# Softmax sums by one reduction on VectorE, copies of the transposed weights on ScalarE

## The chip, the core and the metric

The kernel runs on one core of one Trainium2 chip. The metric is the time of one execution on the device, in microseconds; the median of several executions is compared. The engines named below are TensorE (PE in profile rows, and PEld for its loads of stationary operands), VectorE (DVE), ScalarE (ACT), GpSimd (POOL) and SyncE (SP), which issues most transfers.

## The reference

A block-sparse attention feeds two feed-forward blocks. Batch 4, 8 heads, 576 positions, head width 64, all in float32; cut to what matters:

```python
scores = scale * np.matmul(q, k.transpose(0, 1, 3, 2))
mask_local = (rel >= 0) & (rel < stride)                       # stride = 32, heads 0 to 3
mask_strided = (rel >= 0) & (pos[None, :] % stride == pos[:, None] % stride)   # heads 4 to 7
scores = np.where(masks[None, :, :, :], scores, -1000000000.0)
scores = scores - np.max(scores, axis=-1, keepdims=True)
attn = np.exp(scores)
attn = attn / (np.sum(attn, axis=-1, keepdims=True) + 1e-09)
x = np.matmul(attn, v)                     # then heads side by side: 2304 x 512
h = x @ moe_w_in                           # 512 -> 2048
x = (h * np.tanh(softplus(h))) @ moe_w_out
g, val = x @ moe2_w_gate, x @ moe2_w_val   # 512 -> 1536
out = (g * sigmoid(g) * val) @ moe2_w_out
```

## The kernel before

The attention runs in 24 steps, six per batch: three local steps of 6 tiles of scores 128 x 96, and three strided ones, two of 8 tiles 128 x 64 and one of 6. (A tile holds two blocks of 64 queries, one above the other.) In the first three batches the local steps come first, in the last one the strided ones. Most steps have two halves, written s.0 and s.1.

The order of the work in the attention stage is written out by hand as a list of words, `ORDER`, which one loop turns into instructions. Every engine executes its own instructions in the order of that list. The words of a step s are: `Qs` scores on TensorE, into two PSUM banks ("sc", two buffers, so the scores of step s+1 wait for the maxima of step s); `Ms.h` mask and row maximum on VectorE, one instruction and one reading of its accumulator per tile; `Es.h` exponentials on ScalarE, one per tile, each with its row sum in an accumulator (`accum_out`), whose reading is an instruction of its own; `As` the addition of 1e-9 to the sums on GpSimd; `Rs` the reciprocal on VectorE; `Ns.h` the normalization on GpSimd; `Ts.h` the transposes on TensorE into PSUM; `Cs.h` or `Ds.h` the copy of the transposed weights to SBUF, on VectorE or ScalarE; `Ps` weights times values on TensorE, into the one bank "tp" and, in strided steps, one of "xp"; `Hs` and `Os` the split of the result into a high part (ScalarE) and the rest (VectorE).

Between them stand the words of the first feed-forward block, which starts while the attention still runs: `g` (input matmuls, line 160), `p` (output matmuls), `a`, `b`, `m`, `gh`, `gl`, `y` (what lies between and behind them), `w`, `wh`, `wl`, `wg` (the conversion of weights, four steps each, mostly on VectorE), and `s` (a few matmuls on zeros). `L` and `V` are loads of queries and keys, and of values. Behind the list, from about 118 us, the rest of the two feed-forward blocks follows, three matmuls per product of high and low parts.

Of the kernel before, what the change touches and what calls it, by code (L numbers as in the profile page):

```python
# [62 lines left out]
ORDER = """  # L63
L0
Q0 M0.0 M0.1 E0.0 s4 L1 E0.1
Q1 L2 M1.0 M1.1 A0 E1.0 R0 N0.0 s4
Q2 N0.1 T0.0 M2.1 E1.1 T0.1 A1 M2.0 L3 C0.0 R1
Q3 N1.0 C0.1 E2.1 M3.0 E2.0 N1.1 M3.1 P0 A2 w E3.1 V0 H0 R2 L4 T1.0 T1.1 w s2 C1.0 w D1.1 E3.0 O0 s3 N2.0 N2.1
Q4 w w P1 A3 R3 V1 M4.0 T2.1 wh M4.1 H1 T2.0 N3.0 O1 L5 D2.1
Q5 E4.0 s4 C2.0 P2 N3.1 T3.1 C3.1 w wg E4.1 T3.0 H2 M5.0 w g0.0.0 M5.1 L6  # L70
Q6 A4 R4 w D3.0 N4.0 E5.0 O2 V2 E5.1 w N4.1 M6.1 P3 L7 wh w A5 R5 T4.0 T4.1 M6.0 H3 E6.1 E6.0 g0.0.1 N5.1 C4.0 g0.1.0
Q7 w N5.0 wg O3 D4.1 g0.1.1 T5.0 A6 M7.0 g0.2.0 V3 D5.0 T5.1 w w R6 wh P4 H4 g0.2.1 w D5.1 N6.0 wg M7.1 O4 V4 L8
Q8 E7.0 P5 T6.0 g0.1.2 M8.0 g0.0.2 H5 M8.1 E7.1 O5 N6.1 w E8.0 A7 R7 T6.1 E8.1 C6.1 L9 C6.0 g0.0.3 w b0.0
Q9 P6 N7.1 M9.0 H6 A8 N7.0 wh R8 T7.1 N8.0 V5 M9.1 E9.0 E9.1 L10 g0.1.3 g0.3.0 V6 T7.0 O6
Q10 C7.1 w C7.0 M10.0 M10.1 E10.1 T8.0 E10.0 w C8.0 N8.1 wg L11 w A9 g0.3.1 T8.1 R9
Q11 P7 L12 g0.2.2 H7 N9.0 N9.1 g0.2.3 C8.1 T9.1 M11.0 A10 M11.1 a0.2 R10 b0.1 E11.0 E11.1 V7 C9.1 O7 N10.0 N10.1 A11
T10.1 g0.3.2 T9.0
Q12 M12.1 C10.1 P8 w H8 O8 T10.0 w D9.0 wh L13 g0.3.3 E12.1 g1.0.0 R11 P9 M12.0
Q13 H9 C10.0 N11.0 N11.1 w wg M13.0 M13.1 b0.3 T11.1 D11.1 O9 g1.2.0 g1.0.1 V8 E12.0 g1.2.1 E13.0 A12 w T11.0 L14 V9
P10  # L80
Q14 w R12 L15 M14.0 C11.0 N12.1 H10 E13.1 O10 w N12.0 g1.1.0 g1.1.1 M14.1 E14.0 g1.1.2 P11 T12.0 H11 w E14.1 O11 C12.0
A14 m0.0 V10 wh g1.0.2 w A13 gh0.0 R13 R14 g1.2.2 g1.0.3 g1.1.3 a1.0 N13.0 T12.1 g1.2.3 a1.1 N13.1 g1.3.0 g1.3.1 m0.1
m0.3 w V11 N14.1
Q15 C12.1 gh0.1 wl m0.2 P12 L16 m1.0 H12 gl0.0 w a1.2 T13.0 T13.1 m1.1 D13.0 g1.3.2 gh0.3 p0.2.0 g1.3.3 gl0.1 w gh1.1
M15.0 p0.0.0 p0.0.1 m1.2 C13.1 wh a1.3 M15.1 gh0.2 N14.0 w p0.1.0 wl
Q16 M16.1 T14.1 T14.0 L17 M16.0 m1.3 p0.2.1 w p0.1.1 E15.1 E15.0 wh V12 O12
Q17 gl0.2 A15 E16.0 P13 gl0.3 L18 E16.1 R15 wl C14.0 V13 M17.1 C14.1 p0.0.2 N15.1 H13 M17.0 N15.0 A16 T15.1 p0.1.2
E17.0 O13 p0.2.2 R16 p0.0.3 p0.1.3 p0.2.3 T15.0
Q18 y0.0 y0.2 N16.0 N16.1 M18.1 P14 E17.1 H14 T16.0 A17 R17 C15.0 L19 p0.3.0 E18.1 y0.1 O14 V14 g2.0.0 D15.1 M18.0
p0.3.1 T16.1 C16.0 E18.0 N17.0 P15 N17.1  # L90
Q19 H15 w T17.1 p0.3.2 L20 g2.2.0 M19.1 D17.1 V15 p0.3.3 A18 R18 O15 E19.1 M19.0 gh1.0 T17.0 C16.1 g2.0.1
Q20 C17.0 N18.1 P16 N18.0 L21 y0.3 V16 M20.0 E19.0 T18.1 T18.0 w H16 gh1.3 M20.1 A19 g2.1.0 g2.1.1 D18.1 R19 O16
Q21 N19.0 N19.1 P17 D18.0 T19.0 g2.2.1 w E20.0 H17 g2.0.2 M21.1 T19.1 E20.1 A20 gl1.1 gh1.2 M21.0 g2.2.2 O17 tbl
g2.1.2 R20 gl1.0 g2.0.3 L22
Q22 C19.0 b2.0 P18 N20.0 E21.1 N20.1 H18 T20.1 gl1.2 g2.3.0 w D20.1 E21.0 g2.2.3 V17 A21 g2.1.3 g2.3.1 L23 b2.2 O18
D19.1 M22.1 R21 b2.1 T20.0 g2.3.2 p1.0.0 P19 C20.0 M22.0
Q23 w E22.1 V18 E22.0 N21.0 A22 H19 N21.1 gl1.3 T21.0 M23.1 O19 V19 p1.0.1 E23.1 C21.0 M23.0 g2.3.3 b2.3 p1.1.0 w
E23.0 wh w P20 T21.1 A23 H20 C21.1 p1.0.2 p1.0.3 p1.3.0 m2.3 O20 R22 p1.1.1 p1.1.2 P21 N22.0 T22.0 w wl m2.2 H21 O21
y1.0 R23 p1.3.1 N22.1 gh2.2 N23.1 V20 D22.0 p1.3.2 N23.0 T22.1 D22.1 p1.2.0 gl2.2 p1.2.1 m2.1 P22 T23.0 m2.0 H22
O22 p1.1.3 gh2.0 T23.1 y1.1 gl2.0 wh D23.1 gh2.1 p1.2.2 V21 p1.3.3 p1.2.3 gl2.1 D23.0 P23 V22 H23 O23 gh2.3 wg y1.3  # L100
gl2.3 V23 y1.2
# [1823 lines left out]
```

## Time and profile before

| what | value |
|---|---|
| median of 3 executions | 850.07 us (849.73 to 850.78) |
| the profiled execution | 850.62 us |
| its span, first to last instruction | 848.8 us |
| outside the span | 1.82 us |
| TensorE busy (ends of matmuls modelled) | 840.2 us, 99% |
| VectorE busy | 688.8 us, 81% |
| ScalarE busy | 478.5 us, 56% |
| GpSimd busy | 218.6 us, 26% |

The span is what the rows of the profile cover; what lies around it belongs to the time but to no row. Shares are averages over stages of quite different kinds: the attention stage is the first 118 us of 849.

### The profile page before, as it was taken

How to read it: one execution, taken by the hardware profiler on the slowest of the kernel's cores; microseconds unless marked ns; L12 is line 12 of the kernel's file. 1: busy time of each engine (PE TensorE's matmuls, PEld its weight loads, DVE VectorE, ACT ScalarE, POOL GpSimd, SP SyncE). 2: the span in 40 equal slices, each digit the busy share in tenths (PEclk: the TensorE clock that was granted, in tenths of full speed). 3: DMA queues.
4: the chain of work that ended last, by engine and by line, in shares of the span. 5: the costliest groups of instructions: out<-in, count | busy, mean ns of one | idle time of the engine just before them, and what ended most of it. 6: DMA issues, size and time to landing. Idle time of an engine off the chain costs nothing.

```text
span 848.8 us, 14459 instructions
## 1 busy us (share of the span) xinstructions
PE 840.2 (99%) x5177; PEld 699.7 (82%) x5177; DVE 688.8 (81%) x1442; ACT 478.5 (56%) x1128; POOL 218.6 (26%) x229
## 2 busy tenths in 40 slices
PE   8999999999999999999999999999999999999998
PEld 5778778888888888888888888888888878888886
DVE  6999879687677737687588999999999788677977
ACT  7999965575647547572736535353444534545353
POOL 5552221002000010101222121220205634334253
PEclk9999999999999999999999999999999999999999
DMA  9875353625957494873266655665575777669722
GB/s 283 264 228 167 105 185 158 247 85 115 306 137 218 105 274 138 186 287 144 89 258 223 225 192 198 217 211 206 192 265 181 234 239 222 231 189 249 199 75 100
DMA packets 50184, 166.08 MB, mean 196 GB/s; under 512 B 5440, under 2 KB 9408, under 8 KB 47808
## 3 DMA queue, kind: packets, MB, share of 16 engines
q1 hardware_dynamic: 42480, 133.48, 46.0%
q0 software_dynamic: 6480, 24.12, 12.4%
q10 hardware_dynamic: 1152, 7.55, 2.4%
q8 instruction: 41, 0.67, 0.3%
q14 instruction: 31, 0.25, 0.1%
HBM read 108.51 MB, written 56.62 MB: 195 GB/s over the span
## 4 chain that ended last, share of the span: by engine, by line
PE 92%; DVE 4%; DMA 2%; issue 1%; ACT 1%; POOL 0%; SPq 0%; DVEq 0%; ACTq 0%
PE y L160 23%; PE h L160 8%; PE o L160 8%; PE cX L160 8%; PE cXg L160 7%; PE cXv L160 7%; PE c L160 4%; PE cZ L160 4%; PE cZg L160 4%; PE cZv L160 4%; PE oX L160 3%; PE cY L160 2%; DMA qk<-in_qk_dram 2%; PE xp L599 2%; PE tp L562 2%; PE cYg L160 2%
## 5 line engine op out<-in xcount | busy, mean ns | idle before, releaser
L160 PE MATMUL y<-g,w 128*128 128x512 f32 (+1 forms) x960 | 202.3, 369 | 0.0
L160 PEld LDWEIGHTS y<-g,w 128*128 128x128 f32 x960 | 166.7, 189 | 29.7
L155 POOL TENSOR_TENSOR fs<-k,fs 128x512 fp32r<-128x512 f32 x24 | 37.5, 1569 | 139.9 <-ACT fs L150 127.8
L1143 POOL DMA_DIRECT2D yd<-yv x20 | 16.0, 802 | 187.3 <-ACT yv L1137 187.3
L160 PE MATMUL h<-xh,w 128*128 128x512 f32 (+1 forms) x208 | 61.5, 360 | 0.0
L516 ACT ACTIVATE pt<-pt,sm 128x64 f32<-128x64 f32 (+1 forms) x160 | 55.9, 361 | 3.7 <-DVE sm L502 3.7
L160 PE MATMUL o<-fs,wr 128*128 128x512 f32 x240 | 56.2, 390 | 0.0
L160 PE MATMUL cXg<-T,wr 128*128 128x512 f32 x216 | 54.8, 389 | 0.0
L160 PE MATMUL cXv<-T,wr 128*128 128x512 f32 x216 | 54.8, 389 | 0.0
L160 PEld LDWEIGHTS o<-fs,wr 128*128 128x128 f32 x240 | 44.7, 188 | 9.1
L160 PEld LDWEIGHTS cXv<-T,wr 128*128 128x128 f32 x216 | 40.6, 188 | 8.4
L160 PEld LDWEIGHTS cXg<-T,wr 128*128 128x128 f32 x216 | 40.5, 188 | 8.4
L1581 ACT COPY k<-cXg 128x512 f32<-128x512 f32 x18 | 10.6, 587 | 59.5 <-PE cXg L160 59.3
L160 PEld LDWEIGHTS h<-xh,w 128*128 128x128 f32 x208 | 37.0, 189 | 6.2 <-issue 1.2
L1137 ACT COPY yv<-y 128x512 f32<-128x512 f32 x40 | 23.2, 589 | 28.6 <-PE y L160 26.2
L545 POOL TENSOR_TENSOR pt<-pt,sm 128x192 f32<-128x192 f32 (+2 forms) x48 | 34.1, 730 | 18.1 <-DVE sm L538 13.1
L160 PE MATMUL h<-xl,w 128*128 128x512 f32 (+1 forms) x104 | 36.4, 350 | 0.0
L160 PE MATMUL c<-yh,wr 128*128 128x256 f32 x192 | 35.5, 283 | 0.0
L1590 ACT ACTIVATE k<-k 128x512 f32<-128x512 f32 x27 | 17.1, 633 | 31.1 <-DVE k L1586 31.1
L160 PE MATMUL cX<-xT,w 128*128 128x512 f32 x144 | 34.6, 389 | 0.0
L155 POOL TENSOR_TENSOR fs<-t,fs 128x512 fp32r<-128x512 f32 x20 | 28.5, 1431 | 22.6 <-ACT fs L150 13.6
L155 POOL TENSOR_TENSOR fs<-s,fs 128x512 fp32r<-128x512 f32 x18 | 26.4, 1468 | 27.8 <-ACT fs L150 27.8
(243 smaller groups left out, 2150.6 us busy)
## 6 DMA issues: line engine op xcount, KB each, us to landing
raw<-in_w_dram SPq DMA_DIRECT2D x44, 512.0 KB, 4.7
rawl<-in_w_dram SPq DMA_DIRECT2D x24, 512.0 KB, 4.3
yd<-yv POOLq DMA_DIRECT2D x20, 512.0 KB, 5.9
wr<-wd_p SPq DMA_DIRECT2D x18, 512.0 KB, 4.6
wr<-wd_g_S SPq DMA_DIRECT2D x16, 512.0 KB, 3.4
wr<-wd_v_S SPq DMA_DIRECT2D x14, 512.0 KB, 4.8
wr<-wd_g_W SPq DMA_DIRECT2D x10, 512.0 KB, 6.3
wd_v_W<-wr SPq DMA_DIRECT2D x10, 512.0 KB, 5.4
```

Of the source, the lines that this page charges most:

```text
L155: eng.tensor_tensor(out=lo, in0=src, in1=hi.bitcast(F32), op=ALU.subtract)
L160: nc.tensor.matmul(o, lhsT=lhs, rhs=rhs, start=first and i == 0, stop=last and i == 2, skip_group_check=more)
L516: nc.scalar.activation(out=pt[:, x], in_=pt[:, x], func=AF.Exp, scale=-1.0, bias=sm[:, 0, x:x + 1], accum_out=sm[:, 1, x:x + 1],)
L545: nc.gpsimd.tensor_tensor(out=a, in0=a, in1=sm[:, 1, x].unsqueeze(2).to_broadcast(a.shape), op=ALU.mult)
L562: nc.tensor.transpose(tp[:, 128 * x:128 * x + 128], a, ident)
L599: nc.tensor.matmul(banks[r][64 * h:64 * h + 64, o:o + nq - skip], lhsT=v_t[s][rows, i, 64 * h:64 * h + 64], rhs=ts[rows, c0 + skip:c0 + nq ...
L1137: t = on_act(COPY if nt == 512 else 0.4, clk["pe"], lambda: nc.scalar.copy(dst, p[:, :nt]))
L1143: nc.gpsimd.dma_start(yd[c][:, e0:e + 1], src, **kw)
L1581: read[k, x] = on_act(COPY, max(pe, old), lambda: nc.scalar.copy(t, p))
L1590: s, silu = t, on_act(MISH, ready, lambda: nc.scalar.activation(out=t, in_=t, func=AF.Silu))
```

## The change

The exponentials no longer sum. Word `A` and its function go; word `R` now makes the sums of all tiles of the step with one `tensor_reduce` on VectorE over the exponentials in SBUF, adds 1e-9 there, and then takes the reciprocal. It stands where `R` stood. Every `C` in the list becomes `D`, so that all 40 copies of transposed weights are on ScalarE, 25 of them moved from VectorE. Nothing else in the list moves. Cut to its core (the other lines of the list change in the same way):

```diff
 L0
 Q0 M0.0 M0.1 E0.0 s4 L1 E0.1
-Q1 L2 M1.0 M1.1 A0 E1.0 R0 N0.0 s4
-Q2 N0.1 T0.0 M2.1 E1.1 T0.1 A1 M2.0 L3 C0.0 R1
-Q3 N1.0 C0.1 E2.1 M3.0 E2.0 N1.1 M3.1 P0 A2 w E3.1 V0 H0 R2 L4 T1.0 T1.1 w s2 C1.0 w D1.1 E3.0 O0 s3 N2.0 N2.1
-Q4 w w P1 A3 R3 V1 M4.0 T2.1 wh M4.1 H1 T2.0 N3.0 O1 L5 D2.1
-Q5 E4.0 s4 C2.0 P2 N3.1 T3.1 C3.1 w wg E4.1 T3.0 H2 M5.0 w g0.0.0 M5.1 L6
+Q1 L2 M1.0 M1.1 E1.0 R0 N0.0 s4
+Q2 N0.1 T0.0 M2.1 E1.1 T0.1 M2.0 L3 D0.0 R1
+Q3 N1.0 D0.1 E2.1 M3.0 E2.0 N1.1 M3.1 P0 w E3.1 V0 H0 R2 L4 T1.0 T1.1 w s2 D1.0 w D1.1 E3.0 O0 s3 N2.0 N2.1
+Q4 w w P1 R3 V1 M4.0 T2.1 wh M4.1 H1 T2.0 N3.0 O1 L5 D2.1
+Q5 E4.0 s4 D2.0 P2 N3.1 T3.1 D3.1 w wg E4.1 T3.0 H2 M5.0 w g0.0.0 M5.1 L6
...
                 bias=sm[:, 0, x:x + 1],
-                accum_out=sm[:, 1, x:x + 1],
             )
-    def sums(s):
+    def at_recip(s):
         b, first, g, part = steps[s]
-        r = st[s][1][:, 1]
+        pt, sm = st[s][:2]
+        r = sm[:, 1]
         if first:
-            return r.rearrange("p (h t) -> p h t", h=2)[:, :, :len(part) // 2]
-        return r[:, :len(part)]
-
-    def at_add(s):
-        r = sums(s)
-        nc.gpsimd.tensor_scalar_add(r, r, 1e-9)
-
-    def at_recip(s):
-        r = sums(s)
+            m = len(part) // 2
+            r = r.rearrange("p (h t) -> p h t", h=2)[:, :, :m]
+            pt = pt.rearrange("p (h t) k -> p h t k", h=2)[:, :, :m]
+        else:
+            r = r[:, :len(part)]
+        nc.vector.tensor_reduce(out=r, in_=pt, op=ALU.add, axis=mybir.AxisListType.X)
+        nc.vector.tensor_scalar_add(r, r, 1e-9)
         nc.vector.reciprocal(r, r)
...
-            "A": at_add,
...
-            "C": lambda s, half: at_copy(s, half, nc.vector.tensor_copy),
```

## Rows read from the trace of the kernel before

**Rows 1.** The page: span, then busy us, share of span, count.

```profile
span 848.8 us, 14459 instructions
...
PE 840.2 (99%) x5177; PEld 699.7 (82%) x5177; DVE 688.8 (81%) x1442; ACT 478.5 (56%) x1128; POOL 218.6 (26%) x229
...
```

**Rows 2.** Chain of waits, 0 to 120 us: start, length, what.

```profile
...
7.69 10.75 DMA qk<-in_qk_dram
...
24.19 1.08 issue
...
```

**Rows 3.** Stretches: length; PE, PEld, DVE, ACT, POOL busy (count); clock; DMA share; GB/s.

```profile
...
9.60:18.24 8.64, 7.15 (x135) 5.46 (x135) 8.34 (x57) 8.44 (x42) 5.82 (x11) 1.00 1.04 296
18.24:31.30 13.06, 11.64 (x196) 8.36 (x196) 12.56 (x61) 12.18 (x61) 7.19 (x11) 1.00 0.83 297
31.30:49.00 17.70, 17.70 (x307) 14.34 (x309) 16.39 (x104) 17.28 (x87) 10.31 (x18) 1.00 0.89 282
49.00:70.00 21.00, 21.00 (x304) 16.98 (x296) 19.89 (x91) 20.97 (x73) 8.17 (x12) 1.00 0.49 154
70.00:118.00 48.00, 48.00 (x656) 38.33 (x655) 38.10 (x183) 42.66 (x190) 17.19 (x29) 1.00 0.41 135
...
```

**Rows 4.** Timeline of TensorE: scores of steps 3, 5, 13. Start, length, what.

```profile
...
10.61 0.93 PE L482 MATMUL sc<-qk 64*64 64x64 f32 x32
...
18.57 0.70 PE L482 MATMUL sc<-qk 64*64 64x64 f32 x24 [0.40 <-DMA qk<-in_qk_dram]
...
49.26 0.68 PE L482 MATMUL sc<-qk 64*64 64x96 f32 x23
...
```

**Rows 5.** By line: ns min/median/max; the second DVE copy row is 18.3 to 49 us.

```profile
...
L516 ACT ACTIVATE pt<-pt,sm x160: 331/358/448, 5.8 to 104.3; 128x64 f32<-128x64 f32 x88, 128x96 f32<-128x96 f32 x72
L516 ACT ACTIVATION_READ_ACCUMULATOR pt<-pt,sm x160: 185/194/262, 6.1 to 104.6; 128x1 f32 x160
...
L570 DVE COPY ts<-tp x25: 370/674/692, 10.7 to 105.2; 96x512 f32<-96x512 f32 x9, 96x256 f32<-96x256 f32 x8, 128x512 f32<-128x512 f32 x5, 128x256 f32<-128x256 f32 x3
L570 ACT COPY ts<-tp x15: 365/387/626, 14.8 to 115.7; 96x256 f32<-96x256 f32 x4, 64x256 f32<-64x256 f32 x4, 128x512 f32<-128x512 f32 x3, 96x512 f32<-96x512 f32 x3
...
L570 DVE COPY ts<-tp x9: 370/676/692, 18.8 to 48.9; 96x512 f32<-96x512 f32 x4, 96x256 f32<-96x256 f32 x3, 128x512 f32<-128x512 f32 x2
...
L538 DVE RECIPROCAL sm<-sm x24: 151/191/204, 8.6 to 110.8; 128x6 f32<-128x6 f32 x16, 128x8 f32<-128x8 f32 x8
...
```

**Rows 6.** Groups of VectorE, 0 to 270 us, by form: busy us, mean ns.

```profile
...
L393 DVE TENSOR_SCALAR wt<-raw 128x512 int32<-128x512 int32 x16 | 6.7, 421 | 0.0
...
L826 DVE TENSOR_TENSOR ta<-xh,xl 128x512 f32<-128x512 f32 x8 | 5.5, 686 | 0.0
...
L155 DVE TENSOR_TENSOR w<-wtmp,w 128x512 fp32r<-128x512 f32 x4 | 3.3, 837 | 0.0
...
L155 DVE TENSOR_TENSOR xl<-xp,xh 128x384 fp32r<-128x384 f32 x3 | 1.6, 547 | 0.0
...
```

**Rows 7.** Timeline of VectorE: start, length, what.

```profile
...
8.64 0.18 DVE L538 RECIPROCAL sm<-sm 128x6 f32<-128x6 f32 x1
...
11.71 0.21 DVE L502 CUSTOM_DVE_ANT_0 pt<-sc,cst 128x64 f32<-128x64 f32 x1
...
18.16 0.08 DVE L502 DVE_READ_ACCUMULATOR2_ANT sm<- 128x1 f32 x1
...
48.94 0.08 DVE L502 DVE_READ_ACCUMULATOR2_ANT sm<- 128x1 f32 x1
48.94 0.68 DVE L570 COPY ts<-tp 128x512 f32<-128x512 f32 x1
49.54 0.68 DVE L396 SCALAR_TENSOR_TENSOR wtmp<-raw,wtmp 128x512 int32<-128x512 int32 x1
...
```

**Rows 8.** Timeline of VectorE where an instruction reads the result just before it.

```profile
...
51.92 0.68 DVE L401 SCALAR_TENSOR_TENSOR wtmp<-raw,wtmp 128x512 int32<-128x512 int32 x1
52.63 0.72 DVE L404 SCALAR_TENSOR_TENSOR wtmp<-w,wtmp 128x512 f32<-128x512 f32 x1
...
```

More of the change, by code (lines that the diff above doesn't have):

```diff
@@ L65 @@
 Q0 M0.0 M0.1 E0.0 s4 L1 E0.1
-Q1 L2 M1.0 M1.1 A0 E1.0 R0 N0.0 s4
-Q2 N0.1 T0.0 M2.1 E1.1 T0.1 A1 M2.0 L3 C0.0 R1
-Q3 N1.0 C0.1 E2.1 M3.0 E2.0 N1.1 M3.1 P0 A2 w E3.1 V0 H0 R2 L4 T1.0 T1.1 w s2 C1.0 w D1.1 E3.0 O0 s3 N2.0 N2.1
-Q4 w w P1 A3 R3 V1 M4.0 T2.1 wh M4.1 H1 T2.0 N3.0 O1 L5 D2.1
-Q5 E4.0 s4 C2.0 P2 N3.1 T3.1 C3.1 w wg E4.1 T3.0 H2 M5.0 w g0.0.0 M5.1 L6
-Q6 A4 R4 w D3.0 N4.0 E5.0 O2 V2 E5.1 w N4.1 M6.1 P3 L7 wh w A5 R5 T4.0 T4.1 M6.0 H3 E6.1 E6.0 g0.0.1 N5.1 C4.0 g0.1.0
-Q7 w N5.0 wg O3 D4.1 g0.1.1 T5.0 A6 M7.0 g0.2.0 V3 D5.0 T5.1 w w R6 wh P4 H4 g0.2.1 w D5.1 N6.0 wg M7.1 O4 V4 L8
@@ L73 @@
[L73 to L76, printed above, removed]
+Q1 L2 M1.0 M1.1 E1.0 R0 N0.0 s4
+Q2 N0.1 T0.0 M2.1 E1.1 T0.1 M2.0 L3 D0.0 R1
+Q3 N1.0 D0.1 E2.1 M3.0 E2.0 N1.1 M3.1 P0 w E3.1 V0 H0 R2 L4 T1.0 T1.1 w s2 D1.0 w D1.1 E3.0 O0 s3 N2.0 N2.1
@@ new lines @@
+Q4 w w P1 R3 V1 M4.0 T2.1 wh M4.1 H1 T2.0 N3.0 O1 L5 D2.1
+Q5 E4.0 s4 D2.0 P2 N3.1 T3.1 D3.1 w wg E4.1 T3.0 H2 M5.0 w g0.0.0 M5.1 L6
+Q6 R4 w D3.0 N4.0 E5.0 O2 V2 E5.1 w N4.1 M6.1 P3 L7 wh w R5 T4.0 T4.1 M6.0 H3 E6.1 E6.0 g0.0.1 N5.1 D4.0 g0.1.0
+Q7 w N5.0 wg O3 D4.1 g0.1.1 T5.0 M7.0 g0.2.0 V3 D5.0 T5.1 w w R6 wh P4 H4 g0.2.1 w D5.1 N6.0 wg M7.1 O4 V4 L8
+Q8 E7.0 P5 T6.0 g0.1.2 M8.0 g0.0.2 H5 M8.1 E7.1 O5 N6.1 w E8.0 R7 T6.1 E8.1 D6.1 L9 D6.0 g0.0.3 w b0.0
+Q9 P6 N7.1 M9.0 H6 N7.0 wh R8 T7.1 N8.0 V5 M9.1 E9.0 E9.1 L10 g0.1.3 g0.3.0 V6 T7.0 O6
@@ L77 @@
+Q10 D7.1 w D7.0 M10.0 M10.1 E10.1 T8.0 E10.0 w D8.0 N8.1 wg L11 w g0.3.1 T8.1 R9
+Q11 P7 L12 g0.2.2 H7 N9.0 N9.1 g0.2.3 D8.1 T9.1 M11.0 M11.1 a0.2 R10 b0.1 E11.0 E11.1 V7 D9.1 O7 N10.0 N10.1
 T10.1 g0.3.2 T9.0
-Q12 M12.1 C10.1 P8 w H8 O8 T10.0 w D9.0 wh L13 g0.3.3 E12.1 g1.0.0 R11 P9 M12.0
-Q13 H9 C10.0 N11.0 N11.1 w wg M13.0 M13.1 b0.3 T11.1 D11.1 O9 g1.2.0 g1.0.1 V8 E12.0 g1.2.1 E13.0 A12 w T11.0 L14 V9
-P10
-Q14 w R12 L15 M14.0 C11.0 N12.1 H10 E13.1 O10 w N12.0 g1.1.0 g1.1.1 M14.1 E14.0 g1.1.2 P11 T12.0 H11 w E14.1 O11 C12.0
@@ L82 @@
-A14 m0.0 V10 wh g1.0.2 w A13 gh0.0 R13 R14 g1.2.2 g1.0.3 g1.1.3 a1.0 N13.0 T12.1 g1.2.3 a1.1 N13.1 g1.3.0 g1.3.1 m0.1
+Q12 M12.1 D10.1 P8 w H8 O8 T10.0 w D9.0 wh L13 g0.3.3 E12.1 g1.0.0 R11 P9 M12.0
+Q13 H9 D10.0 N11.0 N11.1 w wg M13.0 M13.1 b0.3 T11.1 D11.1 O9 g1.2.0 g1.0.1 V8 E12.0 g1.2.1 E13.0 w T11.0 L14 V9
+P10
+Q14 w R12 L15 M14.0 D11.0 N12.1 H10 E13.1 O10 w N12.0 g1.1.0 g1.1.1 M14.1 E14.0 g1.1.2 P11 T12.0 H11 w E14.1 O11 D12.0
+m0.0 V10 wh g1.0.2 w gh0.0 R13 R14 g1.2.2 g1.0.3 g1.1.3 a1.0 N13.0 T12.1 g1.2.3 a1.1 N13.1 g1.3.0 g1.3.1 m0.1
@@ L83 @@
 m0.3 w V11 N14.1
-Q15 C12.1 gh0.1 wl m0.2 P12 L16 m1.0 H12 gl0.0 w a1.2 T13.0 T13.1 m1.1 D13.0 g1.3.2 gh0.3 p0.2.0 g1.3.3 gl0.1 w gh1.1
-M15.0 p0.0.0 p0.0.1 m1.2 C13.1 wh a1.3 M15.1 gh0.2 N14.0 w p0.1.0 wl
+Q15 D12.1 gh0.1 wl m0.2 P12 L16 m1.0 H12 gl0.0 w a1.2 T13.0 T13.1 m1.1 D13.0 g1.3.2 gh0.3 p0.2.0 g1.3.3 gl0.1 w gh1.1
+M15.0 p0.0.0 p0.0.1 m1.2 D13.1 wh a1.3 M15.1 gh0.2 N14.0 w p0.1.0 wl
 Q16 M16.1 T14.1 T14.0 L17 M16.0 m1.3 p0.2.1 w p0.1.1 E15.1 E15.0 wh V12 O12
-Q17 gl0.2 A15 E16.0 P13 gl0.3 L18 E16.1 R15 wl C14.0 V13 M17.1 C14.1 p0.0.2 N15.1 H13 M17.0 N15.0 A16 T15.1 p0.1.2
+Q17 gl0.2 E16.0 P13 gl0.3 L18 E16.1 R15 wl D14.0 V13 M17.1 D14.1 p0.0.2 N15.1 H13 M17.0 N15.0 T15.1 p0.1.2
@@ L88 @@
 E17.0 O13 p0.2.2 R16 p0.0.3 p0.1.3 p0.2.3 T15.0
[L89 to L93, printed above, removed]
+Q18 y0.0 y0.2 N16.0 N16.1 M18.1 P14 E17.1 H14 T16.0 R17 D15.0 L19 p0.3.0 E18.1 y0.1 O14 V14 g2.0.0 D15.1 M18.0
@@ L94 @@
+p0.3.1 T16.1 D16.0 E18.0 N17.0 P15 N17.1
+Q19 H15 w T17.1 p0.3.2 L20 g2.2.0 M19.1 D17.1 V15 p0.3.3 R18 O15 E19.1 M19.0 gh1.0 T17.0 D16.1 g2.0.1
+Q20 D17.0 N18.1 P16 N18.0 L21 y0.3 V16 M20.0 E19.0 T18.1 T18.0 w H16 gh1.3 M20.1 g2.1.0 g2.1.1 D18.1 R19 O16
+Q21 N19.0 N19.1 P17 D18.0 T19.0 g2.2.1 w E20.0 H17 g2.0.2 M21.1 T19.1 E20.1 gl1.1 gh1.2 M21.0 g2.2.2 O17 tbl
 g2.1.2 R20 gl1.0 g2.0.3 L22
-Q22 C19.0 b2.0 P18 N20.0 E21.1 N20.1 H18 T20.1 gl1.2 g2.3.0 w D20.1 E21.0 g2.2.3 V17 A21 g2.1.3 g2.3.1 L23 b2.2 O18
@@ L96 @@
-D19.1 M22.1 R21 b2.1 T20.0 g2.3.2 p1.0.0 P19 C20.0 M22.0
-Q23 w E22.1 V18 E22.0 N21.0 A22 H19 N21.1 gl1.3 T21.0 M23.1 O19 V19 p1.0.1 E23.1 C21.0 M23.0 g2.3.3 b2.3 p1.1.0 w
-E23.0 wh w P20 T21.1 A23 H20 C21.1 p1.0.2 p1.0.3 p1.3.0 m2.3 O20 R22 p1.1.1 p1.1.2 P21 N22.0 T22.0 w wl m2.2 H21 O21
+Q22 D19.0 b2.0 P18 N20.0 E21.1 N20.1 H18 T20.1 gl1.2 g2.3.0 w D20.1 E21.0 g2.2.3 V17 g2.1.3 g2.3.1 L23 b2.2 O18
+D19.1 M22.1 R21 b2.1 T20.0 g2.3.2 p1.0.0 P19 D20.0 M22.0
+Q23 w E22.1 V18 E22.0 N21.0 H19 N21.1 gl1.3 T21.0 M23.1 O19 V19 p1.0.1 E23.1 D21.0 M23.0 g2.3.3 b2.3 p1.1.0 w
@@ L99 @@
+E23.0 wh w P20 T21.1 H20 D21.1 p1.0.2 p1.0.3 p1.3.0 m2.3 O20 R22 p1.1.1 p1.1.2 P21 N22.0 T22.0 w wl m2.2 H21 O21
 y1.0 R23 p1.3.1 N22.1 gh2.2 N23.1 V20 D22.0 p1.3.2 N23.0 T22.1 D22.1 p1.2.0 gl2.2 p1.2.1 m2.1 P22 T23.0 m2.0 H22
```

## The prediction

> **What bounds the kernel now.** I read the page, then the chain of waits, then busy time by stretch, then the lines of the softmax, and last the timelines of VectorE and TensorE around the waits. The page [rows 1] says that TensorE is busy for 99% of the span, but the ends of its matmuls are modelled, so the chain has to say whether it really is fed. The chain [rows 2] shows a load of queries and keys that lands at 7.69 + 10.75 = 18.44 us and then, up to 120 us, matmuls that follow each other at their own spacing, with one hole of 1.08 us at 24.19 us that no engine releases. So from about 25 us TensorE is the bound, and its order of work is fixed by the word list. Two things follow. Time taken off ScalarE is worth nothing there by itself, since TensorE waits for nobody. And whatever makes TensorE late at one place in that stage is kept to the end, because nothing behind it has a hole in which to catch up.
>
> The stretches [rows 3] say who is close to becoming that reason. From 31.30 to 49.00 us VectorE is busy for 16.39 of 17.70 us and ScalarE for 17.28. From 9.60 to 18.24 us VectorE has 8.34 of 8.64. ScalarE gets relief from this change and VectorE gets load. The clock is granted in full, 1.00, in all these stretches; I leave it there.
>
> **What ScalarE and GpSimd lose and gain.** 160 readings of an accumulator at 0.194 us [rows 5] go: at most 31.0 us of ScalarE, less in effect because the next exponential starts before a reading ends. 25 copies come to it, between 0.37 and 0.63 us each [rows 5], at most 15.7 us. GpSimd loses 24 tiny additions and gets nothing. None of this is on the path. I cost it at zero; the cover is that TensorE's stream sets the time, and the price without that cover is the ScalarE rival below.
>
> **What VectorE gains and loses, per step.** It loses 25 copies: 14 of 512 columns, 11 of 256 [rows 5]. A copy of 0.68 us is followed 0.60 us later by the next instruction [rows 7], an overlap of 0.08, so the large ones give back 0.60 and the small ones (0.37) about 0.30: 14 x 0.60 + 11 x 0.30 = 11.7 us.
>
> It gains, in each of 24 steps, a sum over 6 x 96, 8 x 64 or 6 x 64 numbers (12, 8 and 4 steps) and an addition on 6 or 8 numbers. No sum of this kind is in the trace. The nearest rows are full-width operations from SBUF [rows 6]: 0.686 us for 512 and 0.547 for 384, a slope of 1.09 ns per column, so 0.756 for 576. The lower bound is the operation that takes two columns at a time, 0.421 for 512; the upper one is the slowest group of that width, 0.837. I take the middle, because the sum reads each column once and in order as those do. For the addition I take the reciprocal's 0.19 [rows 5].
>
> The three operations read each other's results. Where that happens today, the reader starts only after the writer has ended: 51.92 + 0.68 = 52.60, next start 52.63 [rows 8], so a gap of 0.03 in place of an overlap of 0.08. A step's price is thus the sum + 0.03 + 0.19 + 0.03: 1.01, 0.94 and 0.80 us. Over 24 steps that is 12.1 + 7.5 + 3.2 = 22.8 us, and net of the copies VectorE has 11.1 us more.
>
> **Where that becomes TensorE's time.** The scores of step s+1 go to the PSUM banks that the row maxima of step s (VectorE) leave, so VectorE's lateness at the maxima is the gate.
>
> Start. Step 0's reciprocal stood at 8.64 [rows 7] and moves by 1.01. Step 0's normalization, its transposes and, behind them on TensorE, the scores of step 3 move with it: these ran at 10.61 for 0.93 [rows 4], so they end at 12.55. The maxima of step 3 began at 11.71 [rows 7]; they are 0.84 late. Up to the maxima of step 4, steps 2 and 3 add 1.01 + 0.94, the copy of step 1 gives back 0.60, and idle time takes 0.30 [rows 3]: 1.89 late. Those maxima ended at 18.24 [rows 7] and now end at 20.13, while step 5's scores started at 18.57 [rows 4]: TensorE slips 1.56 us. The load that lands at 18.44 is no cover any more.
>
> From there to the maxima of step 12, ended at 49.02 [rows 7]: steps 4 to 11 add 0.94 + 0.80 + 3 x 1.01 + 2 x 0.94 + 0.80 = 7.45. Eight of the nine copies in that stretch [rows 5] stand ahead of it, five large and three small: 3.9 back. VectorE's idle time was 0.50 + 1.31 = 1.81 [rows 3], and I let all of it absorb lateness, since ScalarE and GpSimd, whom it partly waited for, are lighter. So 1.89 + 7.45 - 3.9 - 1.81 = 3.63 late, maxima done at 52.65; step 13's scores started at 49.26 [rows 4], a slack of 0.24. TensorE's slip is then 3.4 us.
>
> After that it stops growing. Twelve sums are left, 11.2 us, against fourteen copies (seven large, seven small, 6.3 us) and idle time of 1.1 + 9.9 = 11.0 us [rows 3]. VectorE recovers, but TensorE has no idle time left to give the 3.4 us back. Weight conversions and the loads that wait for their raw buffers come later too; they are used well behind their conversion, so I cost that at zero.
>
> Sum: 848.8 + 3.4 = 852.2 us of span. The profiled execution took 850.62 us with 1.82 around the span, which would give 854.0; it lies 0.55 above the median, so against the median of 850.07 the forecast is 853.5 us.
>
> Bounds of the price. With the slowest row the sum costs 0.15 more (0.12 for 384): 0.45 more at the start and 1.14 after it, 5.0 us of slip, 855.1. With 0.421 the steps cost 0.72, 0.67 and 0.55; the start comes to 1.04 late (0.7 of slip) and the second ledger to 1.04 + 5.27 - 5.71 = 0.6, so 850.8.
>
> **A rule that speaks otherwise.** In the trace a dependent operation starts 0.03 after its source ends, where an independent one overlaps by 0.08 [rows 8, 7]. The Trainium skill, "VectorE: DVE Perf Modes", section "The DRAIN you can't avoid", says that a semaphore between chained operations costs nothing extra, because the pipe empties after each of them anyway. Here the trace disagrees, by 0.11 us for each such pair; by that rule the sum would be the second rival's. On the other side, the same page's section "The perf-mode tier table (the rule you actually need)" gives a reduce only the slow, one-column mode. No run here shows that yet; by it the lower bound of 0.421 would fall away.
>
> **Rivals.** A: VectorE's new load is hidden, no change, 850.1. For it: 11.0 us of idle time behind 49 us [rows 3]. Against it: the gates at steps 5 and 13 stand ahead of that idle time and have 0.3 and 0.24 us of slack. It holds if the sum runs at two columns at a time and nothing waits in the chain (0.49, 0.45, 0.36 per step): then the maxima of step 4 are 0.36 late and the second ledger is negative.
>
> B: dependent operations keep the overlap. Prices are 0.79, 0.72 and 0.58; the start is 1.23 late, the second ledger adds 5.69 - 5.71, and step 13 slips 1.0: 851.1 us, inside what cannot be told from no change.
>
> C: ScalarE becomes a gate. It now stands at a copy until TensorE has transposed, with the next exponentials queued behind. Step 2's exponentials follow step 0's copies: scores of step 3 at 10.61 + 1.01 = 11.62 mark the end of the transposes, two copies take up to 1.0, and six exponentials at 0.358 [rows 5] end at 14.8; VectorE could sum them at about 12.55 + 8 x 0.21 = 14.2. That is 0.5 us lost once, and up to 3 if several steps repeat it: 854 to 856.5. Against it, the exponentials come closer together without the readings.
>
> D, the other side: ScalarE's relief feeds TensorE sooner. It can act only behind 18.44 us, where TensorE lacks 13.06 - 11.64 = 1.42 us up to 31.30 [rows 3], and 0.13 at step 5. All of it would give 848.5 us, and 1.08 of it is the hole that no engine releases. It decides only if VectorE's price per step is below what copies and idle time return, 0.45 us or so.
>
> **Chances.** What a measurement can tell from no change is 0.2%, 1.7 us: 848.4 to 851.8. Forecast (slip of 2 to 5.5 us) 0.50; A 0.17; B 0.15, four fifths of it inside the bound; C 0.12; D 0.06, half of it past the bound. Slower: 0.50 + 0.12 + 0.03 = 0.65. Same: 0.17 + 0.12 + 0.03 = 0.32. Faster: 0.03. Range 849.9 to 856.0: it leaves out D, part of A and the upper half of C. The likeliest case's own range is 852.0 to 855.6.
>
> **What would show it.** Step 0's sum right behind the maxima of step 1, near 0.76 us long, the reciprocal some 1.0 us later than 8.64; scores of step 5 near 20.1 instead of 18.57; scores of step 13 near 52.7 instead of 49.26; VectorE above 17.2 us busy in the stretch that was 31.30 to 49.00; ScalarE well below its 17.28; and from there on the same stream shifted by one constant. Wrong: sums near 0.42, a chain without gaps, idle time of ScalarE in front of the exponentials, or TensorE late at a transpose or at the split of an output instead of at the scores.

## The result, and the profile after

The changed kernel takes 860.49 us (860.22 to 861.18, 4 runs) against 849.98 us (849.73 to 850.78, 4 runs) in the same comparison: a ratio of 1.012, 95% interval 1.0108 to 1.0133. It is slower by 10.5 us; 853.5 was forecast, with 856.0 as the upper end. The profiled execution took 860.35 us, with a span of 858.3 us. The busy times of its page, beside [rows 1]:

```profile
PE 844.0 (98%) x5177; PEld 701.2 (82%) x5177; DVE 698.5 (81%) x1465; ACT 474.8 (55%) x993; POOL 211.2 (25%) x205
```

VectorE has 9.7 us more, ScalarE only 3.7 less. **The price of a step** is as forecast: 1.0 us from the start of the sum to the end of the reciprocal, with gaps of 0.03 and 0.04 and not overlaps. VectorE of the changed kernel, groups by form, 0 to 120 us, and then its timeline, in the place of [rows 7]:

```profile
L534 DVE TENSOR_REDUCE sm<-pt 128x6 f32<-128x576 f32 x12 | 8.9, 743 | 0.0
...
L534 DVE TENSOR_REDUCE sm<-pt 128x8 f32<-128x512 f32 x8 | 5.4, 677 | 0.0
...
L534 DVE TENSOR_REDUCE sm<-pt 128x6 f32<-128x384 f32 x4 | 2.2, 542 | 0.0
```

```profile
8.62 0.75 DVE L534 TENSOR_REDUCE sm<-pt 128x6 f32<-128x576 f32 x1
9.40 0.17 DVE L535 TENSOR_SCALAR sm<-sm 128x6 f32<-128x6 f32 x1
9.61 0.19 DVE L536 RECIPROCAL sm<-sm 128x6 f32<-128x6 f32 x1
```

**What it becomes.** The stretches of [rows 3] from the second on, same columns, of the changed kernel:

```profile
18.24:31.30 13.06, 12.03 (x173) 8.66 (x170) 12.31 (x64) 9.36 (x35) 5.09 (x7) 0.74 0.73 239
31.30:49.00 17.70, 16.20 (x270) 12.38 (x270) 16.37 (x102) 15.50 (x58) 8.64 (x11) 1.00 0.69 220
49.00:70.00 21.00, 19.28 (x257) 14.74 (x255) 19.54 (x87) 18.07 (x59) 8.73 (x13) 1.00 0.69 206
70.00:118.00 48.00, 47.44 (x689) 37.89 (x688) 42.48 (x211) 42.82 (x136) 11.18 (x16) 1.00 0.43 137
```

In the last three stretches TensorE had no idle time at all [rows 3]; now it has 1.50, 1.72 and 0.56 us. VectorE was to be fuller from 31.30 to 49.00 and is not: 16.37 of 17.70, where it had 16.39. It idles as long as before while TensorE waits. And the granted clock, left at 1.00 in the forecast, is 0.74 in the second stretch.

The chain of waits from 34 us on (start, length, what) shows what stands between two pieces of TensorE's work:

```profile
37.28 0.38 ACT xh L150 x3
37.67 1.60 ACT pt L516 x7
...
39.40 0.64 ACT pt L516 x2
40.04 0.74 ACT ts L568 x2
...
40.83 0.94 PE xp L597 x24
...
53.52 0.62 DVE xl L155 x2
54.15 0.33 DVE wtmp L393
54.48 0.47 DVE sm L534
54.98 0.18 DVE sm L535
55.18 0.19 DVE sm L536
```

Once it is ScalarE: a split, nine exponentials and two copies, then TensorE. Once it is VectorE: a split, a weight conversion and the three new instructions, then a row maximum. In [rows 2] the chain between 25 and 120 us is TensorE alone.

How late TensorE is at the same piece of work, against the kernel before (start of the scores of a step minus its start there, in us, from the timelines; "end" is the last input matmul of the attention stage, 117.73 us before). The columns to the right belong to the experiments below. Each column is one execution. How far such a one scatters shows in the column of steps 12 to 23: up to step 11 that kernel's list is the old one, and yet it stands at +0.48 and then at -0.64.

| scores of step | before at | changed | sums only | copies only | readings kept | steps 0 to 3 | steps 0 to 11 | steps 12 to 23 | more on zeros |
|---|---|---|---|---|---|---|---|---|---|
| 5 | 18.57 | 1.81 | 2.24 | 0.23 | 1.86 | 1.24 | 1.82 | 0.48 | 2.14 |
| 6 | 22.30 | 4.67 | 2.73 | 2.55 | 3.77 | 3.53 | 4.68 | 0.47 | 2.47 |
| 9 | 35.34 | 4.50 | 4.00 | 1.27 | 3.87 | 2.76 | 4.51 | -0.64 | 3.59 |
| 13 | 49.26 | 6.07 | 6.83 | 3.83 | 7.03 | 2.76 | 6.08 | -0.64 | 5.15 |
| 15 | 62.14 | 7.81 | 9.64 | 5.16 | 9.11 | 2.76 | 7.41 | 0.55 | 6.92 |
| 20 | 86.03 | 7.99 | 10.41 | 6.50 | 10.90 | 2.75 | 7.40 | 0.71 | 7.07 |
| end | 117.73 | 9.53 | 11.78 | 6.67 | 12.64 | 2.76 | 7.41 | 2.40 | 8.61 |

The changed kernel's lateness goes up over the stage, most of all up to step 15 and again behind step 20, to 9.53 us; 9.5 is the difference of the spans. Behind the stage nothing is added.

### The profile page after: what moved, and what is told of

It reads as the page before. It is cut to its first block, busy times and chain, and to the rows that moved or that the text cites. A ratio compares the mean times of both kernels' runs of the same rounds, so it can differ in the third digit from the quotient of the medians.

```text
span 858.3 us, 14325 instructions
## 1 busy us (share of the span) xinstructions
PE 844.0 (98%) x5177; PEld 701.2 (82%) x5177; DVE 698.5 (81%) x1465; ACT 474.8 (55%) x993; POOL 211.2 (25%) x205
## 4 chain that ended last, share of the span: by engine, by line
PE 89%; DVE 7%; ACT 2%; issue 1%; POOL 1%; DVEq 0%; POOLq 0%; ACTq 0%
PE y L160 23%; PE o L160 8%; PE cX L160 8%; PE cXg L160 7%; PE cXv L160 7%; PE h L160 6%; PE c L160 4%; PE cZ L160 4%; PE cZg L160 4%; PE cZv L160 3%; PE oX L160 3%; PE cY L160 2%; PE cYg L160 2%; PE cYv L160 2%; PE oZ L160 1%; PE sc L482 1%
## 5 line engine op out<-in xcount | busy, mean ns | idle before, releaser
L516 ACT ACTIVATE pt<-pt,sm 128x64 f32<-128x64 f32 (+1 forms) x160 | 44.1, 360 | 4.0 <-DVE sm L502 4.0
L502 DVE CUSTOM_DVE_ANT_0 pt<-sc,cst 128x64 f32<-128x64 f32 (+1 forms) x160 | 28.2, 232 | 7.2 <-PE sc L482 7.0
```

Source lines behind the costliest of these rows:

```text
L502: nc.vector.tensor_tensor_reduce(pt[:, x], sc[h][:, t * w:(t + 1) * w], m, -0.125, 3.0e38, ALU.add, ALU.min, accum_out=sm[:, 0, x:x + 1],)
L516: nc.scalar.activation(out=pt[:, x], in_=pt[:, x], func=AF.Exp, scale=-1.0, bias=sm[:, 0, x:x + 1],)
```

## The experiments

Beside each, the time of the kernel before in the same comparison. Of an edit of the list one line is shown; the others change in the same way.

**The two parts, each alone.** Sums only: the reductions, but the copies stay where they were; the list is that of the kernel before without its words `A`. Copies only: every `C` becomes `D`, the exponentials keep their sums and GpSimd its additions.

```diff
 # sums only, against the changed kernel
-Q2 N0.1 T0.0 M2.1 E1.1 T0.1 M2.0 L3 D0.0 R1
+Q2 N0.1 T0.0 M2.1 E1.1 T0.1 M2.0 L3 C0.0 R1
 # copies only, against the kernel before
-Q2 N0.1 T0.0 M2.1 E1.1 T0.1 A1 M2.0 L3 C0.0 R1
+Q2 N0.1 T0.0 M2.1 E1.1 T0.1 A1 M2.0 L3 D0.0 R1
```

> The sums by one reduction on VectorE as in the changed kernel, but the 25 copies stay on VectorE. Theory V (VectorE's extra work of about 1.0 us per step is what TensorE waits for): with nothing given back by the copies VectorE carries 22.8 us more instead of 11.1, so slower than the changed kernel's 860.5 us, 864 to 872. Theory S (the copies on ScalarE, with exponentials and splits queued behind them, are most of the loss): most of the loss goes, 853 to 856. Theory K (TensorE's clock, granted at half around 20 to 28 us, is most of it): unchanged by this edit in kind, 859 to 861.

> All 40 copies on ScalarE, the sums by the exponentials as before. Theory V: VectorE is 11.7 us lighter, no loss, 850 to 851 us. Theory S: ScalarE, already busy for 17.28 of 17.70 us between 31 and 49 us, gets 25 copies on top, 855 to 862 us. Theory K: no loss unless TensorE idles at the start, 850 to 852.

Measured, against 849.94: sums only 862.5 us (1.0134 to 1.0164), copies only 858.1 us (1.0074 to 1.0104). Sums only lies between two of its ranges (859 to 861 and 864 to 872), copies only in the one of theory S. Each part alone costs most of the whole, 12.6 and 8.2 us; together they cost 10.5. So moving the copies does give back 2.1 us once the sums are on VectorE, where by the prediction's ledger 11.7 us of VectorE's time left with them. The other half of the account stands on ScalarE. Copies only, the last three stretches:

```profile
31.30:49.00 17.70, 15.15 (x268) 12.07 (x260) 11.76 (x86) 17.16 (x85) 9.26 (x14) 1.00 0.70 217
49.00:70.00 21.00, 19.70 (x309) 15.86 (x308) 17.26 (x74) 20.82 (x84) 9.55 (x15) 1.00 0.66 210
70.00:118.00 48.00, 47.23 (x639) 37.26 (x638) 35.30 (x196) 47.34 (x200) 14.00 (x26) 1.00 0.40 132
```

VectorE has 5.9 us to spare from 31.30 to 49.00, and yet TensorE loses 2.55 us there. ScalarE is the full one, 17.16, 20.82 and 47.34; it had 17.28, 20.97 and 42.66 [rows 3].

**ScalarE's load in the changed kernel.** The exponentials accumulate again, into a tile that nobody reads, so that the readings of [rows 5] come back as mere load.

```diff
                 bias=sm[:, 0, x:x + 1],
+                accum_out=spare[:, x:x + 1],
             )
```

> The changed kernel, but its exponentials still accumulate row sums into a spare tile that nobody reads, so ScalarE has the 160 readings of accumulators back and nothing else moves. If VectorE's chain is what passes the lateness on (ScalarE waits for TensorE for 12 us in 0 to 128 us and has room): 860 to 862 us. If ScalarE's own time is on the way too, now that it has all 40 copies: 864 us or more.

Measured: 864.26 us against 850.19 (1.0149 to 1.0179), 3.8 us above the changed kernel. ScalarE's time counts. A reading makes the next exponential start some 0.09 us later (below), 15 us over 160 of them, and these cost 3.8; the table shows where: nothing more up to step 9, then 0.96 by step 13, 2.9 by step 20 and 3.1 at the end, growing where ScalarE is fullest. The last two stretches of that run:

```profile
49.00:70.00 21.00, 18.96 (x252) 14.74 (x252) 18.52 (x88) 20.25 (x87) 8.37 (x13) 1.00 0.59 189
70.00:118.00 48.00, 46.27 (x661) 36.38 (x660) 40.54 (x204) 46.15 (x195) 10.13 (x15) 1.00 0.40 127
```

**Place or load of the copies.** Copies only, with each moved copy right behind its transposes in the list.

```diff
-Q8 E7.0 P5 T6.0 g0.1.2 M8.0 g0.0.2 H5 M8.1 E7.1 O5 N6.1 w E8.0 A7 R7 T6.1 E8.1 D6.1 L9 D6.0 g0.0.3 w b0.0
+Q8 E7.0 P5 T6.0 D6.0 g0.1.2 M8.0 g0.0.2 H5 M8.1 E7.1 O5 N6.1 w E8.0 A7 R7 T6.1 D6.1 E8.1 L9 g0.0.3 w b0.0
```

> All copies on ScalarE with the row sums still in the exponentials' accumulators, as in the run with the copies alone, but each moved copy stands in the list right behind its transposes instead of where VectorE's copy stood. If the copies are late because of their place behind exponentials: 852 to 855 us. If ScalarE is simply full (its busy share with the copies alone was 97 to 99% from 34 to 118 us): 857 to 859 us, as before the move.

Measured: 860.94 us against 849.7 (1.008 to 1.0137). That is above both ranges. An earlier place gains nothing; the median is even 2.8 us above the run with the copies where they stood, though the intervals overlap. ScalarE now waits 3.3 us for transposes ahead of its copies, up to 128 us, where it waited 1.4 us in copies only. That a copy placed ahead also pushes exponentials back is likely, but not shown.

**VectorE's time, a little less and a little more.** Without the addition of 1e-9; with one more reduction per step ahead of the sum; with the same reduction behind the reciprocal.

```diff
 # no addition
-        nc.vector.tensor_scalar_add(r, r, 1e-9)
 # one more reduction, ahead of the sum; in the third variant this line stands behind the reciprocal
+        nc.vector.tensor_reduce(out=spare[:, :5], in_=cst.rearrange("p (a k) -> p a k", k=96), op=ALU.add, axis=mybir.AxisListType.X)
         nc.vector.tensor_reduce(out=r, in_=pt, op=ALU.add, axis=mybir.AxisListType.X)
```

> The changed kernel without the addition of 1e-9 in each step, so that a step's price on VectorE falls from 1.00 to about 0.80 us. Theory V: the slip at the scores of step 5 falls by some 0.6 to 0.8 us and the whole by 2 to 4, 856.5 to 858.5 us. Theory S: 860 us, within 0.5 of the changed kernel. Theory K: 860, or 858 if TensorE's shorter wait keeps the clock.

> The changed kernel with one more VectorE reduction per step, over 5 x 96 constants into a spare tile that nobody reads, ahead of the sum: some 0.6 us each, 14.4 us over 24 steps, in front of the reciprocal and of all that VectorE does behind it. The sums' own 22.8 us cost 11.8 us of span when they were put in alone, 0.52 per us; at that rate and at the 0.36 per us that leaving out the addition returned, 865.5 to 868 us. If VectorE's time is hidden in idle time: 860 to 861.

> The same extra reduction right behind the reciprocal: VectorE is as long occupied, but the reciprocal, the normalization and the transposes of the step don't wait for it. If the loss comes from the later reciprocal (latency of the step's chain): under 863 us. If it comes from VectorE's occupancy, the later maxima and with them the next scores: within 1 us of the variant with the reduction ahead, 865.5 to 868 us.

Measured: 858.02 us without the addition (1.0074 to 1.0108, against 849.94); 869.13 (1.018 to 1.0246) with the reduction ahead and 867.82 (1.0167 to 1.0222) with it behind, both against 849.7. The first is 2.5 us below the changed kernel for 24 x (0.17 + 0.03) = 4.8 us of VectorE, 0.5 per us. (Its profiled execution, the slowest of four, is 7.91 us late at the end in place of 9.53: 0.34 per us.) The extra reductions take 0.645 and 0.609 us, from the first and the second variant's groups:

```profile
L535 DVE TENSOR_REDUCE spare<-cst 128x5 f32<-128x480 f32 x22 | 14.2, 645 | 0.0
```

```profile
L538 DVE TENSOR_REDUCE spare<-cst 128x5 f32<-128x480 f32 x22 | 13.4, 609 | 0.0
```

They make 24 x 0.645 = 15.5 and 24 x 0.609 = 14.6 us, which cost 8.6 and 7.3 us of time: 0.56 and 0.50 per us. The first is 1.1 us above the range that it was given, the two are 1.3 apart where 1 was allowed. Behind the reciprocal, where neither the step's normalization nor its transposes wait for it, the extra work still costs 85% as much. So what counts is mostly that VectorE is occupied, which delays all that stands behind in its list, and not that the step's own sums come late.

**Which steps.** The change in steps 0 to 3, 0 to 11, or 12 to 23 only; the other steps as before. Words `A`, `C` and `D` are those of the kernel that the step belongs to. The code of 0 to 11, against the changed kernel:

```diff
                 bias=sm[:, 0, x:x + 1],
+                **({} if s < 12 else {"accum_out": sm[:, 1, x:x + 1]}),
...
-        nc.vector.tensor_reduce(out=r, in_=pt, op=ALU.add, axis=mybir.AxisListType.X)
-        nc.vector.tensor_scalar_add(r, r, 1e-9)
+        if s < 12:
+            nc.vector.tensor_reduce(out=r, in_=pt, op=ALU.add, axis=mybir.AxisListType.X)
+            nc.vector.tensor_scalar_add(r, r, 1e-9)
```

> The change in steps 0 to 3 only. The recorded prediction has 1.56 us of slip at step 5 from these and says that idle time of VectorE absorbs lateness behind it, so that at step 13 0.1 to 0.3 us would be left, but TensorE keeps what it has slipped: 851.5 to 852 us. If the fall of TensorE's clock behind the start matters too, as in the changed kernel, where the slip was 4.5 us at step 9: 853 to 855 us.

> The change in steps 0 to 11 only; steps 12 to 23 sum, add and copy as the kernel before. Prediction's own step (TensorE's slip is made ahead of about 49 us and stays constant behind it): the whole loss is here, 859.5 to 861 us. Loop theory (lateness runs round TensorE, ScalarE, VectorE and GpSimd and each further step adds to it): the slip at the scores of step 13 is about the 6.1 us that the changed kernel had there, and nothing is added behind, so 855.5 to 857 us.

> The change in steps 12 to 23 only; steps 0 to 11 as the kernel before. Prediction's own step (VectorE has 11 us of idle time behind 49 us, which hides the twelve sums left): 849.5 to 851 us, no change. Loop theory (VectorE's idle time is spent in waits inside the loop, so a longer step price is passed to TensorE there too): the 3.5 us that the changed kernel's slip grew behind step 13, so 852.5 to 854.5 us.

Measured: 853.83 us for steps 0 to 3 (851.77 to 855.92; 1.0024 to 1.0055, against 849.7), 857.46 for 0 to 11 (1.0068 to 1.0102; 0.5 above the nearer of its two ranges), 853.19 for 12 to 23 (852.31 to 858.27; 1.003 to 1.007; both against 850.19). The two halves cost 7.3 and 3.0 us, 10.3 of the whole change's 10.5: the loss adds up over the stage. The slips tell more. From steps 0 to 3 alone, TensorE is 2.76 us late at step 9 and exactly that at the end: a delay that is there is neither worked off nor does it breed. It grows only where changed steps go on (the last words of step 11 stand in the lines of steps 13 and 14, so 0 to 11 still gains 1.3 us there). And in steps 12 to 23, for which the forecast had no loss because VectorE had 11.0 us of idle time there [rows 3], TensorE goes from 0.64 us ahead at step 13 to 2.40 late at the end: 3.0 us, as in the medians.

**The clock.** More matmuls on zeros where TensorE waits: 8 ahead of the weights times values of step 1, 5 ahead of the scores of step 5.

```diff
-Q4 w w P1 R3 V1 M4.0 T2.1 wh M4.1 H1 T2.0 N3.0 O1 L5 D2.1
-Q5 E4.0 s4 D2.0 P2 N3.1 T3.1 D3.1 w wg E4.1 T3.0 H2 M5.0 w g0.0.0 M5.1 L6
+Q4 s8 w w P1 R3 V1 M4.0 T2.1 wh M4.1 H1 T2.0 N3.0 O1 L5 D2.1
+s5 Q5 E4.0 s4 D2.0 P2 N3.1 T3.1 D3.1 w wg E4.1 T3.0 H2 M5.0 w g0.0.0 M5.1 L6
```

> The changed kernel with 13 more matmuls on zeros where TensorE waits before its clock falls: 8 ahead of the weights-times-values of step 1, 5 ahead of the scores of step 5. Theory K: the granted clock stays at 1.00 from 18 to 28 us, the slip at the scores of step 6 falls from 4.67 to about 2.5 us, and the end comes 1 to 2.3 us earlier, 858.2 to 859.5. Theories V and S: the waits behind 28 us are the same and only that part moves; if the clock had cost nothing, 860.5.

Measured: 859.36 us against 849.94 (1.0092 to 1.0122), 1.1 below the changed kernel. Stretches 18 to 22 and 22 to 28 us of the changed kernel, then of this one:

```profile
18.00:22.00 4.00, 2.97 (x55) 2.38 (x53) 3.93 (x25) 3.65 (x14) 2.13 (x3) 0.68 0.82 249
22.00:28.00 6.00, 6.00 (x91) 4.12 (x89) 5.39 (x24) 2.56 (x10) 1.71 (x3) 0.64 0.64 212
```

```profile
18.00:22.00 4.00, 3.87 (x61) 2.71 (x62) 3.93 (x25) 3.65 (x14) 1.96 (x3) 1.00 0.75 237
22.00:28.00 6.00, 4.80 (x96) 3.57 (x95) 5.93 (x29) 4.77 (x19) 2.17 (x3) 1.00 0.72 236
```

The granted clock stays at 1.00, and TensorE is 2.47 us late at step 6 in place of 4.67. Of these 2.2 us, half is gone again by step 9 (3.59 against 4.50), and 0.92 is left at the end. In this kernel the clock is a part of the loss, about 1 us, not its cause: the profiled execution with the copies right behind their transposes had 1.00 from 9.60 to 118 us, and its TensorE is 7.99 us late at the end all the same. But it scatters the times of other variants. Of steps 12 to 23 the four executions with a mean granted clock of 0.999 or 1.000 took 852.31 to 853.19 us, the three with 0.996 to 0.998 took 855.51 to 858.27; of steps 0 to 3 the two with 0.998 took 851.77 and 852.14, the eight with 0.995 or 0.996 took 853.31 to 855.92. Whether the clock made those late or went down because they waited longer is not shown.

**The addition on GpSimd before.** The kernel before without its words `A`.

```diff
-Q2 N0.1 T0.0 M2.1 E1.1 T0.1 A1 M2.0 L3 C0.0 R1
+Q2 N0.1 T0.0 M2.1 E1.1 T0.1 M2.0 L3 C0.0 R1
```

> The kernel before without the addition of 1e-9 to the row sums (left out: the constant; each sum holds the 1 of its own maximum). GpSimd loses 24 tiny instructions. If TensorE's stream is the bound and waits for nobody, 849.5 to 850.5 us, the same. If the chain from the exponentials over addition, reciprocal and normalization to the transposes is on the way in the kernel before too, 848.5 us or less.

Measured: 850.9 us against 850.19 (1.0001 to 1.002), 0.7 above, within what counts as no change and above the 850.5 that was expected at most. Where TensorE waits for nobody, these additions taken off GpSimd are worth nothing, in line with what the prediction says of time off other engines. Nothing that was tried beats the kernel before.

## Why the prediction was right in direction and wrong in size

**Right: the price.** 1.01, 0.94 and 0.80 us per step were forecast; the sums take 0.74, 0.68 and 0.54, the addition 0.17 to 0.18 and the reciprocal 0.19 to 0.20, with gaps of 0.03 to 0.04. The sum over 512 columns takes 0.677 us, as long as the slower row of that width (0.686) and not 0.421. With that the lower bound falls, and with the gaps rival B (the overlap of 0.08 stays). Neither explains the miss. (Its own prices make the last twelve sums 11.4 us and not 11.2, which changes nothing.)

**Right: the start.** Scores of step 3 at 11.68, 11.62 forecast; reciprocal at 9.61, 8.64 + 1.01 = 9.65 forecast. The maxima of step 4 end at 20.8 where 20.13 stands in the prediction, 0.5 of it because one instruction of a weight conversion ahead of them took 1.20 us where it had taken 0.71. Slip at step 5: 1.81 against 1.56. TensorE of the changed kernel, beside [rows 4], and one row of its VectorE:

```profile
17.17 0.55 DVE L155 TENSOR_TENSOR xl<-xp,xh 128x384 fp32r<-128x384 f32 x1
...
17.82 0.92 PE L597 MATMUL xp<-ts,v 96*64 96x64 f32 x24 [2.10 <-ACT pt L516]
...
20.38 0.44 PE L482 MATMUL sc<-qk 64*64 64x64 f32 x2 [0.85 <-PE tp L560]
21.00 0.91 PE L482 MATMUL sc<-qk 64*64 64x64 f32 x22 [0.18 <-DVE sm L502]
21.85 1.89 PE L1685 MATMUL wp<-wz 128*128 128x512 bf16 x4
```

The same two pieces of the kernel before:

```profile
15.31 0.54 DVE L155 TENSOR_TENSOR xl<-xp,xh 128x384 fp32r<-128x384 f32 x1
...
15.96 0.92 PE L599 MATMUL xp<-ts,v 96*64 96x64 f32 x24 [0.76 <-PE sc L482]
```

**Not foreseen: the wait of 2.10 us.** The row puts it down to ScalarE's exponentials, but the last of these had ended at 17.58. The matmuls, weights times values of step 1, write the one bank that VectorE's split of step 0 reads, and that split ended at 17.72, 0.1 us ahead of them. Before, it ended at 15.85, again 0.1 us ahead; the distance is the same in every trace here but that of sums only. So this wait is for VectorE, at a place that the prediction lists under "Wrong": "TensorE late at a transpose or at the split of an output". It doesn't decide the slip at step 5, since the scores there wait another 0.85 us, until 0.1 us behind the fourth maximum of step 4 (20.27).

**Wrong, a little: "the clock is granted in full, 1.00, in all these stretches; I leave it there".** Behind the wait of 2.10 us the granted clock fell to 0.50, the lower of its two levels, and the wait of 0.85 us lies already in that time:

```profile
17.00:19.40 2.40, 1.58 (x30) 1.42 (x30) 2.37 (x6) 2.20 (x9) 0.62 (x1) 1.00 0.60 163
19.50:22.00 2.50, 1.47 (x26) 1.17 (x26) 2.50 (x21) 2.35 (x9) 2.13 (x3) 0.50 0.86 294
```

Four matmuls on zeros took 1.89 us in place of 1.04. Of the hole of 1.08 us at 24.19 [rows 2] nothing is left; the chain shows no issue of that length there. Where it stood, from step 6 to step 7, the slip falls from 4.67 to 3.19; with the clock held at 1.00 the slip at step 9 is 0.91 us less.

**The step that failed: idle time as a cushion.** The prediction let "all of it absorb lateness", 1.81 us up to step 13 and 11.0 us behind it, from which followed 3.4 us of slip and "After that it stops growing". To see whether VectorE's idle time was used up, the same work has to be compared: from the scores of step 5 to those of step 13, and from there to the "end" of the table. Columns as in [rows 3]; the kernel before, the changed one, sums only:

```profile
18.57:49.26 30.69, 29.61 (x518) 22.93 (x521) 28.88 (x162) 29.39 (x146) 17.43 (x28) 1.00 0.86 287
49.26:117.73 68.47, 68.47 (x938) 54.78 (x929) 57.73 (x269) 63.22 (x261) 25.10 (x40) 1.00 0.44 140
```

```profile
20.38:55.33 34.95, 32.63 (x517) 24.53 (x518) 32.12 (x173) 27.42 (x99) 15.45 (x20) 0.92 0.72 231
55.33:127.26 71.93, 69.98 (x939) 55.15 (x929) 62.51 (x286) 62.36 (x194) 21.66 (x29) 1.00 0.44 137
```

```profile
20.81:56.09 35.28, 31.15 (x517) 23.07 (x518) 34.45 (x181) 24.98 (x92) 16.48 (x20) 1.00 0.71 231
56.09:129.51 73.42, 70.23 (x939) 54.98 (x929) 67.69 (x300) 57.12 (x181) 21.03 (x29) 1.00 0.41 134
```

VectorE idled for 1.81 and 10.74 us before, and for 2.83 and 9.42 in the changed kernel: of 12.55 us 0.3 were used up, and with 8.0 us more of work on VectorE the two parts take 7.7 us longer. In sums only, where VectorE is fullest, it idles for 0.83 and 5.73, so 6.0 us were used up. But in the second part it has 9.96 us more to do, less than the 10.74 us that it idled there before, and yet 5.73 stay idle and TensorE loses 4.95 us (6.83 to 11.78 in the table). No copy has moved to ScalarE in that run, so ScalarE's load is not the reason. What VectorE waits for are scores and splits. That these come late because VectorE was late before is read from the waits and from the order of the list; no run breaks that loop. The waits of the changed kernel, 0 to 128 us (engine, for whom, us, times, longest), have such pairs in both directions:

```profile
ACT xh L150 <- PE xp L597: 12.4, 10, 2.9
...
DVE pt L502 <- PE sc L482: 7.0, 10, 1.9
DVE xl L155 <- ACT xh L150: 5.8, 7, 1.5
...
PE sc L482 <- DVE sm L502: 0.9, 3, 0.4
```

By the experiments the parts are: steps 0 to 3, 2.8 us of slip by the end (1.56 forecast); steps 4 to 11, 7.41 - 2.76 = 4.65 (1.84 forecast); steps 12 to 23, 2.1 (what the whole change has beyond 0 to 11) to 3.0 (alone), none forecast. Without any cushion the prediction's ledger would have had 1.56, 3.65 and 4.9 us, 10.1 in all. That is near the 9.53 by luck, since the last term is too large and the first two too small.

**Wrong: ScalarE at zero.** "None of this is on the path" fails twice: the copies alone cost 8.2 us, with VectorE 11.7 us lighter by the ledger, and bringing the readings back costs 3.8. TensorE's stream does not cover what is put on ScalarE; 17.28 of 17.70 us busy [rows 3] was the warning. Rival C had that engine right, but its price, "0.5 us lost once, and up to 3 if several steps repeat it", is far below the 8.2. Rivals A (hidden) and D (faster) are out.

**Open.** Why so little of VectorE's idle time takes up load is argued and not tested, as said above. How the 4.65 us of the middle divide over the single waits was not taken apart: sums and copies, each alone, lose 4.6 and 3.6 us between the scores of steps 5 and 13, and both together 4.3, so they cannot be added.

## What to carry to other kernels

When engines that are nearly full feed each other in a ring, don't count the idle time of one as a cushion: it can be a wait for another that will shift too. Here at most 6.0 of 12.55 us took up load. Price a load by a rate, measured with a small dose; here an extra us of VectorE cost about half a us of time, with less and with more of it, ahead of the dependent step or behind it. Relief of one engine by loading another that is as full gives back only part: here 2.1 us for 11.7.
